# mLSTM and two expert layers on one Trainium2 core: the denominators' absolute values in PSUM, and other durations and ready times in the planner

## The chip, the cores and the metric

The kernel runs on one core of a Trainium2 chip. A core has a matrix engine (TensorE, PE in the rows; PEld is its weight load), three engines for elementwise work (VectorE, DVE; ScalarE, ACT; GpSimd, POOL) and a queue of DMA issues (SyncE, SP). The metric is the device time of one execution in microseconds (us); the time of a kernel is the median of several executions.

## The reference

An mLSTM over 4 batches and 8 heads, 768 steps, 40 columns a head; its output goes through two layers of the form `activation(x @ w_in) @ w_out`.

```python
for t in range(S):
    m_new = np.maximum(f_gate[:, :, t] + m, i_gate[:, :, t])
    f_stab = np.exp(f_gate[:, :, t] + m - m_new)
    i_stab = np.exp(i_gate[:, :, t] - m_new)
    C = f_stab * C + i_stab * np.einsum('bhd,bhe->bhde', vt, kt)
    n = f_stab * n + i_stab * kt
    h_tilde = np.einsum('bhde,bhe->bhd', C, qt)
    nq = np.einsum('bhd,bhd->bh', n, qt)
    denom = np.maximum(np.abs(nq), 1.0)
    y[:, :, t] = sigmoid(o_gate) * h_tilde / denom
...
h = x @ w_in;  x = (h - np.tanh(h)) @ w_out            # first layer, 320 -> 2048 -> 320
h = x @ w_in;  x = quadratic_relu(h) @ w_out           # second layer
```

## The kernel before

The 768 steps are cut into 6 chunks of 128. A *job* is one chunk of one batch, 24 in all, numbered chunk by chunk. A job loads q, k, v and o (`qkraw`, `nat`, `q3`) and its rows of the decay factors (`fb`, `gb`), and computes: decays by two scans on DVE (`d`, L456), scores on PE (`t_s`, L469, from job 12 on L485), scores times decays on DVE (L489), the matmul with the carried state (`t_n`, L521) and the matmul with the values (`t_n`, L530, the *value matmul* below). Then comes the chain that the change touches: the denominators of `t_n` through an absolute value on ACT (L537), a maximum with 1 on DVE (L538) and a reciprocal on DVE (L539), all 128x8; o times the reciprocal on POOL (L540); the product with `t_n` on DVE (`x`, L547); its transposes on PE (`t_x`, L552), and the splitting of `t_x` into high and low halves (L602 to L607). The state for the next chunk is built from `t_c` (L559) on ACT and DVE (L567 to L576).

From job 12 on q and k are split into halves before the scores (`xf`): ACT scales (L480), POOL subtracts for one half, DVE for the other (L482).

The layers run in 24 steps of 16 over blocks of 512 tokens (a *step* is one block with 128 columns of the hidden layer): 8 matmuls `h` (L630), an activation on ACT (L648) and DVE (L649), the high part on ACT (`gh`, L660) and the low part on DVE (`gl`, L661), and two steps later 12 matmuls `a` (L681) that read `gh` and `gl`. The first 8 steps of the first block (`wide`) have 3 `h` (L623) and 4 `a` in full precision; their weights `wf` are put together on ACT (`wf`, `cvb`, L316) and DVE (L318, L320), two instructions on each engine for a weight tile. The steps of the first layer run between the jobs of the next block; the second layer has no jobs beside it.

The order is made by a planner (`Plan`). Every operation has an engine, a duration in ns and a priority; `schedule` starts operations one after another on each engine by their ready time and priority, and the order of starts is the order in which they are issued. All engines then work off their instructions in that order, whatever the chip's real times are. An operation with `lock=True` takes its turn on one resource that DVE and POOL share in the plan. Idle time of PE before the first step is filled with dummy matmuls (`spare`, L769).

The decay factors of the later chunks go through DRAM: DVE ends them by a scan (`gr`, L381) and a memset (`fr`, L384), SP stores them (`gr_d`, `fr_d`), and SP loads them broadcast (`gb`, `fb`). On POOL, `gb` is copied in part to `gw` (L512, L513) and multiplied into `q3` (L506, L508), which L521 reads.

Of the kernel before, what the change touches and what calls it, by code (L numbers as in the profile page):

```python
# [69 lines left out]
class Op:  # L70
    __slots__ = ("eng", "ns", "prio", "fn", "allocs", "bufs", "preds", "succs", "left", "est", "start", "end", "seq", "out", "fill", "lock")


class Plan:
# [20 lines left out]
    def op(self, eng, ns, prio, fn, r=(), w=(), out=None, lock=False):  # L95
# [3 lines left out]
        o.bufs, o.fill, o.lock = [], 0, lock  # L99
# [114 lines left out]
def act(n, more=0):  # L214
    return 186 + n / 1.2 + 60 * more
# [12 lines left out]
def mlstm_moe_moe(ctx: ExitStack, tc: tile.TileContext, ig, fg, qk, qk3, q3, nat, w1, w2, cst, out):  # L228
# [107 lines left out]
    def gates(g, prio):  # L336
# [11 lines left out]
        op("DVE", 60, prio, lambda: nc.vector.tensor_copy(m_sb[:, 0:1], carry[:, g:g + 1]), [("carry", g)], [m_sb])  # L348
# [53 lines left out]
    def job(n, at, ld):  # L402
# [499 lines left out]
```

## Time and profile before

| | us |
|---|---|
| median of 3 executions | 820.48 (819.66 to 822.74) |
| the profiled execution | 822.96 |
| its span, first to last instruction | 821.2 |
| PE busy | 806.8 |
| DVE busy | 601.8 |
| ACT busy | 431.1 |
| POOL busy | 156.3 |

The span is the profiled execution less 1.8 us around it. Matmuls are pipelined, and a matmul that follows another closely is counted from its own start, so PE's busy time can hold short stalls; the waits of the rows below are times in which PE had nothing in flight.

### The profile page before, as it was taken

Reading aid. Unit: us, or ns where it says so; the run is one execution under the profiler, and the core shown is the slowest. Engines: PE = TensorE matmul, PEld = TensorE weight load, DVE = VectorE, ACT = ScalarE, POOL = GpSimd, SP = SyncE. Lnnn points to the kernel's source line nnn. Section 1 sums busy time; section 2 is a strip of 40 time slices with the busy share of each in tenths; the row PEclk is TensorE's granted clock in tenths of the full one; section 3 lists DMA queues with packets and bytes.
Section 4 is the critical chain, followed back from the end, with each engine's and each line's share of the span. In section 5 each row is a group of like instructions: output and inputs, shape, how many; then the busy total and the mean of one; then the engine's idle time right before and its main releaser. Section 6 shows DMA issues by size and latency. Waiting matters only on the chain.

```text
span 821.2 us, 15205 instructions
## 1 busy us (share of the span) xinstructions
PE 806.8 (98%) x6030; PEld 704.4 (86%) x6034; DVE 601.8 (73%) x922; ACT 431.1 (53%) x804; POOL 156.3 (19%) x179
## 2 busy tenths in 40 slices
PE   8999999999999999999999999999999999999998
PEld 6566887888988888888899989999999999999997
DVE  6999988879998898998666675565655655655654
ACT  4866764675676766654355543443433533433332
POOL 3253122315333332532020100100100100100000
PEclk9999999999999999999999999999999999999999
DMA  8889266576777767772263130100200000000000
GB/s 291 288 255 289 97 189 163 156 238 169 205 191 208 203 167 196 195 221 74 77 179 105 55 71 1 39 34 1 71 1 1 32 1 1 33 1 1 33 1 32
DMA packets 62978, 93.65 MB, mean 114 GB/s; under 512 B 4700, under 2 KB 45500, under 8 KB 62908
## 3 DMA queue, kind: packets, MB, share of 16 engines
q1 hardware_dynamic: 62860, 92.66, 38.7%
q8 instruction: 47, 0.77, 0.4%
q14 instruction: 23, 0.19, 0.1%
q10 hardware_dynamic: 48, 0.03, 0.0%
HBM read 78.88 MB, written 13.80 MB: 113 GB/s over the span
## 4 chain that ended last, share of the span: by engine, by line
PE 83%; DMA 7%; DVE 7%; issue 2%; ACT 1%; SPq 1%; POOL 0%; ACTq 0%; DVEq 0%; POOLq 0%
PE a L681 37%; PE h L630 36%; PE h L623 3%; DMA w_d<-w 3%; DMA w<-in_w_dram 2%; PE t_n L530 1%; PE t_n L521 1%; DVE d L456 1%; PE t_s L485 1%; DVE gl L661 1%; PE t_s L469 1%; DMA nat<-in_nat_dram 1%; PE t_x L552 1%; DMA gb<-gr_d 1%; PE t_c L559 1%
## 5 line engine op out<-in xcount | busy, mean ns | idle before, releaser
L630 PE MATMUL h<-x,w 128*128 128x512 f32 x1472 | 382.4, 396 | 0.0
L681 PE MATMUL a<-w,gh 128*128 128x320 f32 x1472 | 330.4, 310 | 0.2
L630 PEld LDWEIGHTS h<-x,w 128*128 128x128 f32 x1472 | 265.8, 188 | 44.9
L681 PEld LDWEIGHTS a<-w,gh 128*128 128x128 f32 x1472 | 253.7, 188 | 15.3 <-issue 0.6
L681 PE MATMUL a<-w,gl 128*128 128x320 f32 x736 | 227.9, 310 | 1.5 <-DVE gl L661 1.5
L661 DVE TENSOR_TENSOR gl<-g,gh 128x512 fp32r<-128x512 f32 x184 | 138.4, 753 | 82.1 <-ACT gh L660 80.9
L660 ACT CAST gh<-g 128x512 fp32r<-128x512 f32 x184 | 113.8, 619 | 114.6 <-DVE g L657 70.9
L681 PEld LDWEIGHTS a<-w,gl 128*128 128x128 f32 x736 | 138.5, 188 | 2.2 <-DVE gl L661 1.8
L655 ACT ACTIVATE g<-g,half 128x512 f32<-128x512 f32 x96 | 69.4, 723 | 127.7 <-DVE g L653 127.4
L657 DVE TENSOR_TENSOR g<-h,g 128x512 f32<-128x512 f32 x96 | 66.4, 692 | 73.5 <-ACT g L655 72.7
L649 DVE TENSOR_TENSOR g<-h,g 128x512 f32<-128x512 f32 x88 | 60.1, 682 | 31.8 <-ACT g L648 31.5
L648 ACT ACTIVATE g<-h 128x512 f32<-128x512 f32 x88 | 52.4, 596 | 57.2 <-PE h L630 56.9
L739 POOL TENSOR_TENSOR x<-xl,x 128x512 fp32r<-128x512 f32 x18 | 23.5, 1332 | 275.4 <-ACT x L734 275.0
L653 DVE TENSOR_SCALAR g<-h 128x512 f32<-128x512 f32 x96 | 66.2, 690 | 1.9 <-PE h L630 1.8
L456 DVE TENSOR_TENSOR_SCAN d<-fb,scan_id 128x512 f32<-128x512 f32 x40 | 56.9, 1432 | 0.0
L482 POOL TENSOR_TENSOR xf<-qkraw,xf 120x1024 fp32r<-120x1024 f32 x12 | 30.8, 2571 | 53.8 <-ACT xf L480 45.6
L480 ACT ACTIVATE xf<-qkraw,cs 120x512 fp32r<-120x512 f32 x48 | 32.4, 716 | 9.5 <-PE t_s L485 9.4
L489 DVE TENSOR_TENSOR d<-t_s,d 128x512 f32<-128x512 f32 x48 | 31.7, 679 | 4.6 <-PE t_s L485 3.4
L540 POOL TENSOR_TENSOR nat<-nat,dn 128x320 f32<-128x320 f32 x24 | 22.7, 947 | 58.3 <-DVE dn L539 58.3
L316 ACT ACTIVATE cvb<-w,half 128x704 bf16<-128x704 int8 x32 | 30.1, 941 | 4.7 <-DVE w L318 3.9
L496 POOL TENSOR_TENSOR nat<-nat,isT 128x328 f32<-128x328 f32 x24 | 20.3, 860 | 57.2 <-DMA nat<-in_nat_dram 27.4
L316 ACT ACTIVATE w<-w,half 128x704 f32<-128x704 int8 x24 | 22.6, 941 | 6.0 <-DMA w_d<-w 5.0
(98 smaller groups left out, 684.9 us busy)
## 6 DMA issues: line engine op xcount, KB each, us to landing
w<-in_w_dram SPq DMA_DIRECT2D x32, 703.6 KB
nat<-in_nat_dram SPq DMA_DIRECT2D x24, 484.0 KB
qkraw<-in_qk_dram SPq DMA_DIRECT2D x24, 480.0 KB
fb<-fr_d SPq DMA_DIRECT2D x40, 256.0 KB
w_d<-w SPq DMA_DIRECT2D x16, 352.0 KB
w<-w_d SPq DMA_DIRECT2D x16, 352.0 KB
qkraw<-in_qk_dram SPq DMA_DIRECT2D x24, 160.0 KB
xr_d<-xo SPq DMA_DIRECT2D x24, 160.0 KB
```

The source lines that it names most:

```text
L316: op("ACT", 935, prio, lambda o=o, y=y: nc.scalar.activation(o(), x(), AF.Relu, bias=rebase, scale=y * 2.0 ** 27), [t, "half"], [u if y > ...
L456: op("DVE", dve(1024), p, lambda o=dk[u][0], i=f[u][0]: nc.vector.tensor_tensor_scan(out=o(), data0=i(), data1=scan_id, initial=0.0, op0=A ...
L480: op("ACT", act(512, 1), at(u - 1), lambda raw=raw, t=t, z=z, cols=cols: nc.scalar.activation(t[:, cols], raw[:, cols], AF.Copy, scale=cs[ ...
L630: op("PE", pe(n), prio, lambda i=i, c=c, s=s: nc.tensor.matmul(p[:, :n], w[:, c:c + 128], x[:, s, :n], start=(i == 0), stop=(i == 7)), [(w ...
L648: op("ACT", act(n), prio + 0.5 - FFN, lambda: nc.scalar.activation(t[:, :n], p[:, :n], AF.Tanh), [p], [t])
L649: op("DVE", dve(n), prio + 0.5 - FFN, lambda: nc.vector.tensor_tensor(out=t[:, :n], in0=p[:, :n], in1=t[:, :n], op=ALU.subtract), [p, t], [t])
L653: op("DVE", dve(n), prio + 0.5 - FFN, lambda: nc.vector.tensor_scalar(t[:, :n], p[:, :n], -1.0, 1.0, op0=ALU.max, op1=ALU.min), [p], [t])
L655: op("ACT", act(n, 1), prio + 0.5 - FFN, lambda: nc.scalar.activation(t[:, :n], t[:, :n], AF.Square, bias=half[:, 0:1], scale=0.5), [t, "h ...
L657: op("DVE", dve(n), prio + 0.5 - FFN, lambda: nc.vector.tensor_tensor(out=t[:, :n], in0=p[:, :n], in1=t[:, :n], op=ALU.max), [p, t], [t])
L660: op("ACT", act(n), prio + 1 - FFN, lambda: nc.scalar.copy(gh[:, :n], t[:, :n]), [t], [gh])
L661: low = lambda e: e.tensor_tensor(out=gl[:, :n], in0=t[:, :n], in1=gh[:, :n].bitcast(F32), op=ALU.subtract)
L681: op("PE", pe(DM) if gl is not None else 2 * pe(DM, 128, 2), prio, lambda A=A, r=r, a=a, c=c, i=i, dt=dt: nc.tensor.matmul(A[:, 0:DM], a[: ...
```

## The change

There are three parts. The absolute value on ACT is written to columns 384 to 391 of the PSUM bank of `t_n` instead of to the SBUF tile `dn`, and the maximum on DVE reads it there and writes `dn`; the reciprocal stays in SBUF. The planner's durations are replaced for several operations (POOL's, three small DVE copies, ACT's operations with a scale, the value matmul). And `slack` is new: the ready time of a PE operation is put off by 600 ns after its last input for `t_x` and by 400 ns for the scores from job 12 on.

```diff
+SLACK = [600.0, 400.0, 0.0]
...
-                    s.est = max(s.est, o.end + (self.FAR if s.eng == "PE" else self.NEAR))
+                    s.est = max(s.est, o.end + (self.FAR + s.slack if s.eng == "PE" else self.NEAR))
...
-    return 186 + n / 1.2 + 60 * more
+    return 186 + n / 1.2 + 110 * more
...
-                        t[:, h * L:(h + 1) * L], start=True, stop=True), [t], [sp[u]])
+                        t[:, h * L:(h + 1) * L], start=True, stop=True), [t], [sp[u]], slack=SLACK[1])
...
-        op("POOL", pool(H * E1), at(1), lambda: nc.gpsimd.tensor_tensor(
+        op("POOL", 740, at(1), lambda: nc.gpsimd.tensor_tensor(
...
-                op("POOL", 530, at(1), lambda: nc.gpsimd.tensor_copy(gw[:, 0:2], g[:, 0:2, L - 1]), G, [gw])
+                op("POOL", 190, at(1), lambda: nc.gpsimd.tensor_copy(gw[:, 0:2], g[:, 0:2, L - 1]), G, [gw])
...
-        op("PE", 355 + 2 * H * 38, at(4), pv, [dk[0][1], dk[1][1], V], [p])
+        op("PE", 900, at(4), pv, [dk[0][1], dk[1][1], V], [p], slack=SLACK[2] if n >= FIRST else 0.0)
...
-        op("ACT", 180, at(5), lambda: nc.scalar.activation(dn.t, pn()[:, :, D], AF.Abs), [p], [dn])
-        op("DVE", 170, at(5), lambda: nc.vector.tensor_scalar_max(dn.t, dn.t, 1.0), [dn], [dn])
+        op("ACT", 180, at(5), lambda: nc.scalar.activation(p[:, 384:384 + H], pn()[:, :, D], AF.Abs), [p], [(p, "d")])
+        op("DVE", 175, at(5), lambda: nc.vector.tensor_scalar_max(dn.t, p[:, 384:384 + H], 1.0), [(p, "d")], [dn])
...
-                px[:, k * L:(k + 1) * L], x[:, k * 128:(k + 1) * 128], ident), [x, (x, "z"), "cs"], [px])
+                px[:, k * L:(k + 1) * L], x[:, k * 128:(k + 1) * 128], ident), [x, (x, "z"), "cs"], [px], slack=SLACK[0] if n >= FIRST else 0.0)
```

With one line more at the top, a line of the code after has a number one higher than the same line before (L538 is L539 after).

The order changes nearly everywhere in the first 420 us. Three places follow.

**The start, DVE, from the product x of job 2 to that of job 3.** `dn_528` before and `dn_520` after are job 3's denominators; L318 and L320 (L319 and L321 after) put weight tiles together. Before:

```order
L547 TENSOR_TENSOR x_108<-t_n_395,nat_156 128x320
L318 TENSOR_TENSOR wf_384<-wf_384,cvb_442 128x704
L320 SCALAR_TENSOR_TENSOR wf_384<-w64_256,wf_384 128x704
L538 TENSOR_SCALAR dn_528<-dn_528 128x8
L539 RECIPROCAL dn_528<-dn_528 128x8
L547 TENSOR_TENSOR x_108<-t_n_489,nat_209 128x320
```

After:

```order
L548 TENSOR_TENSOR x_108<-t_n_395,nat_154 128x320
L321 SCALAR_TENSOR_TENSOR wf_283<-w64_171,wf_283 128x704
L319 TENSOR_TENSOR wf_383<-wf_383,cvb_429 128x704
L539 TENSOR_SCALAR dn_520<-t_n_482 128x8
L540 RECIPROCAL dn_520<-dn_520 128x8
L321 SCALAR_TENSOR_TENSOR wf_383<-w64_256,wf_383 128x704
L319 TENSOR_TENSOR wf_447<-wf_447,cvb_522 128x704
L321 SCALAR_TENSOR_TENSOR wf_447<-w64_285,wf_447 128x704
L548 TENSOR_TENSOR x_108<-t_n_482,nat_209 128x320
```

Three weight instructions moved in between the reciprocal and the product of job 3; by that product DVE has done six of them where it had done four.

**Job 8, DVE, from its maximum to its product x, and SP's issues for jobs 8 and 9.** `g_1650` is the activation of the step then in work, `gl_1680` its low part, `fb_1565` the decays of job 9, `xo` the output of the first block. DVE before:

```order
L538 TENSOR_SCALAR dn_1634<-dn_1634 128x8
L649 TENSOR_TENSOR g_1650<-h_1567,g_1650 128x512
L539 RECIPROCAL dn_1634<-dn_1634 128x8
L456 SCALAR_TENSOR_TENSOR d_1671<-fb_1565,scan_id_73 128x512
L661 TENSOR_TENSOR gl_1680<-g_1650,gh_1669 128x512
L692 STREAM_TRANSPOSE xo_1624<-a_617 128x10x32
L692 STREAM_TRANSPOSE xo_1624<-a_624 128x10x32
L547 TENSOR_TENSOR x_108<-t_n_1577,nat_1025 128x320
```

DVE after:

```order
L539 TENSOR_SCALAR dn_1620<-t_n_1552 128x8
L662 TENSOR_TENSOR gl_1625<-g_1550,gh_1605 128x512
L540 RECIPROCAL dn_1620<-dn_1620 128x8
L693 STREAM_TRANSPOSE xo_1614<-a_651 128x10x32
L457 SCALAR_TENSOR_TENSOR d_1644<-fb_1526,scan_id_73 128x512
L457 SCALAR_TENSOR_TENSOR d_1656<-fb_1542,scan_id_73 128x512
L330 TENSOR_TENSOR w2_1496<-wf_447,w2_1496 128x704
L693 STREAM_TRANSPOSE xo_1614<-a_656 128x10x32
L693 STREAM_TRANSPOSE xo_1614<-a_661 128x10x32
L577 SCALAR_TENSOR_TENSOR C_1683<-C_797,gw_1522,t_c_1608 120x123 x2
L650 TENSOR_TENSOR g_1685<-h_1632,g_1685 128x512
L548 TENSOR_TENSOR x_108<-t_n_1552,nat_1015 128x320
```

The low part of the step that is in work stands ahead of both scans after, and behind a scan before. SP before (`w64` is a weight tile of 703.6 KB for the second layer; `gb_1435` and `gb_1480` belong to jobs 8 and 9):

```order
L282 DMA gr_d_79<-gr_1382 32x128
L282 DMA fr_d_78<-fr_1075 32x128
L282 DMA nat_1412<-in_nat_dram 128x968
L282 DMA w64_1421<-in_w2_dram 128x5629
L282 DMA gb_1435<-gr_d_79 40x3x128
L282 DMA fb_1444<-fr_d_78 128x4x128
L282 DMA fb_1457<-fr_d_78 128x4x128
L282 DMA gb_1435<-gr_d_79 40x3x128
L282 DMA gb_1435<-gr_d_79 40x2x128
L282 DMA gb_1480<-gr_d_79 40x3x128 x2
L282 DMA gb_1480<-gr_d_79 40x2x128
```

SP after:

```order
L283 DMA gr_d_79<-gr_1402 32x128
L283 DMA fr_d_78<-fr_1029 32x128
L283 DMA nat_1422<-in_nat_dram 128x968
L283 DMA gb_1441<-gr_d_79 40x3x128
L283 DMA fb_1451<-fr_d_78 128x4x128
L283 DMA fb_1456<-fr_d_78 128x4x128
L283 DMA gb_1441<-gr_d_79 40x3x128
L283 DMA gb_1441<-gr_d_79 40x2x128
L283 DMA gb_1475<-gr_d_79 40x3x128 x2
L283 DMA gb_1475<-gr_d_79 40x2x128
L283 DMA fr_1489<-in_fg_dram 32x128
L283 DMA ig_1493<-in_ig_dram 32x128
```

The weight load moved from ahead of the `gb` loads to behind them.

**Job 14, PE, from the step whose activation DVE works off last before the product x (`h_3058` before, `h_3116` after) to `t_x`.** Before:

```order
L630 MATMUL h_3058<-x1_1710,w9_931 128x512 x8
L681 MATMUL a_2647<-w7_1910,gh_2980 128x320 x2
L681 MATMUL a_2647<-w7_1910,gl_3017 128x320
L681 MATMUL a_2657<-w7_1910,gh_2980 128x320 x2
L681 MATMUL a_2657<-w7_1910,gl_3017 128x320
L681 MATMUL a_2661<-w7_1910,gh_2980 128x320 x2
L681 MATMUL a_2661<-w7_1910,gl_3017 128x320
L681 MATMUL a_2678<-w7_1910,gh_2980 128x320 x2
L681 MATMUL a_2678<-w7_1910,gl_3017 128x320
L630 MATMUL h_3111<-x1_1710,w10_966 128x512 x2
L552 MATMUL t_x_3119<-cs_72,x_108 128x128 x3
```

After:

```order
L631 MATMUL h_3116<-x1_1733,w10_985 128x512 x8
L682 MATMUL a_2634<-w8_840,gh_3074 128x320 x2
L682 MATMUL a_2634<-w8_840,gl_3129 128x320
L682 MATMUL a_2642<-w8_840,gh_3074 128x320 x2
L682 MATMUL a_2642<-w8_840,gl_3129 128x320
L682 MATMUL a_2657<-w8_840,gh_3074 128x320 x2
L682 MATMUL a_2657<-w8_840,gl_3129 128x320
L682 MATMUL a_2674<-w8_840,gh_3074 128x320 x2
L682 MATMUL a_2674<-w8_840,gl_3129 128x320
L631 MATMUL h_3163<-x1_1733,w11_1031 128x512 x8
L553 MATMUL t_x_3180<-cs_72,x_108 128x128 x3
```

Between the two stand 12 `a` and 2 `h` before, 12 `a` and 8 `h` after.

## Rows read from the trace of the kernel before

**Rows 1.** Busy time by stretch: us, PE, PEld, DVE, ACT, POOL, clock, DMA, GB/s.

```profile
32.90:120.00 87.10, 86.86 (x682) 63.66 (x682) 80.61 (x127) 64.25 (x122) 23.80 (x33) 1.00 0.69 212
200.00:420.00 220.00, 214.60 (x1914) 189.96 (x1913) 190.25 (x285) 130.05 (x262) 72.34 (x73) 1.00 0.62 172
```

**Rows 2.** What PE waited for, whole span: us in total, times, longest.

```profile
PE t_x L552 <- DVE x L547: 4.2, 4, 1.5
PE a L681 <- DVE gl L661: 1.5, 1, 1.5
...
PE t_s L485 <- DVE x L607: 1.1, 2, 0.9
...
PE t_n L521 <- POOL q L508: 0.2, 1, 0.2
```

**Rows 3.** The same columns as rows 1, around 130 us.

```profile
128.00:131.10 3.10, 1.46 (x8) 0.99 (x8) 3.10 (x6) 0.20 (x1) 1.02 (x2) 0.99 0.36 81
131.10:134.50 3.40, 3.40 (x14) 3.26 (x14) 2.54 (x7) 1.21 (x3) 0.31 (x2) 0.51 0.95 222
```

**Rows 4.** Timeline at job 8: start us, us, engine, instruction, idle before and releaser.

```profile
127.10 2.14 DVE L456 TENSOR_TENSOR_SCAN d<-fb,scan_id 128x512 f32<-128x512 f32 x1
...
127.43 0.72 POOL L540 TENSOR_TENSOR nat<-nat,dn 128x320 f32<-128x320 f32 x1
...
129.16 0.66 DVE L661 TENSOR_TENSOR gl<-g,gh 128x512 fp32r<-128x512 f32 x1
...
129.88 0.41 PE L681 MATMUL a<-w,gl 128*128 128x320 f32 x1 [1.54 <-DVE gl L661]
```

**Rows 5.** The maximum and the reciprocal: durations in ns, least/median/most; POOL's L482 beside them.

```profile
L538 DVE TENSOR_SCALAR dn<-dn x24: 140/172/2400, 14.8 to 401.5; 128x8 f32<-128x8 f32 x24
...
L539 DVE RECIPROCAL dn<-dn x24: 193/203/205, 15.0 to 401.7; 128x8 f32<-128x8 f32 x24
...
L482 POOL TENSOR_TENSOR xf<-qkraw,xf x12: 2387/2464/3107, 151.0 to 385.2; 120x1024 fp32r<-120x1024 f32 x12
```

**Rows 6.** Groups by line: busy us, mean ns of one.

```profile
L648 ACT ACTIVATE g<-h 128x512 f32<-128x512 f32 x88 | 52.4, 596 | 57.2 <-PE h L630 56.9
...
L538 DVE TENSOR_SCALAR dn<-dn 128x8 f32<-128x8 f32 x24 | 19.9, 829 | 4.9 <-ACT dn L537 4.7
```

**Rows 7.** Timeline at jobs 12, 14 and 17: POOL and DVE, and PE's wait.

```profile
198.56 3.01 DVE L661 TENSOR_TENSOR gl<-g,gh 128x512 fp32r<-128x512 f32 x1
...
238.79 0.67 DVE L649 TENSOR_TENSOR g<-h,g 128x512 f32<-128x512 f32 x1
...
240.01 0.52 PE L552 MATMUL t_x<-cs,x 128*128 128x128 f32 x3 [0.80 <-DVE x L547]
...
292.12 2.37 DVE L538 TENSOR_SCALAR dn<-dn 128x8 f32<-128x8 f32 x1
```

**Rows 8.** The chain that ended last, pieces: start us, us, what.

```profile
108.97 5.09 DMA w<-in_w_dram
114.07 6.60 DMA gb<-gr_d
...
146.41 1.84 PE h L630 x8
148.25 1.75 PE a L681 x12
```

**Rows 9.** Timeline of the start, ACT, DVE and PE.

```profile
29.84 0.93 ACT L316 ACTIVATE cvb<-w,half 128x704 bf16<-128x704 int8 x1
...
31.20 0.49 DVE L547 TENSOR_TENSOR x<-t_n,nat 128x320 f32<-128x320 f32 x1 [0.83 <-POOL nat L540]
31.61 0.88 DVE L318 TENSOR_TENSOR wf<-wf,cvb 128x704 int32<-128x704 f32 x1
...
32.87 7.99 PE L623 MATMUL h<-xf,wf 128*128 128x512 f32 x18
```

**Rows 10.** Timeline of PE at job 8's matmul with the carried state.

```profile
122.73 0.45 PE L521 MATMUL t_n<-C,q 80*128 80x82 f32 x2 [0.15 <-POOL q L508]
```

More of the change, by code (lines that the diff above doesn't have):

```diff
@@ L70 @@
 class Op:
-    __slots__ = ("eng", "ns", "prio", "fn", "allocs", "bufs", "preds", "succs", "left", "est", "start", "end", "seq", "out", "fill", "lock")
+    __slots__ = ("eng", "ns", "prio", "fn", "allocs", "bufs", "preds", "succs", "left", "est", "start", "end", "seq", "out", "fill", "lock", "slack")
 class Plan:
@@ L93, in buf, with op @@
         return b
-    def op(self, eng, ns, prio, fn, r=(), w=(), out=None, lock=False):
+    def op(self, eng, ns, prio, fn, r=(), w=(), out=None, lock=False, slack=0.0):
         o = Op()
@@ L98, in op @@
         o.allocs, o.preds, o.succs = [], set(), []
-        o.bufs, o.fill, o.lock = [], 0, lock
+        o.bufs, o.fill, o.lock, o.slack = [], 0, lock, slack
         key = lambda x: x if isinstance(x, tuple) else (x, None)
@@ L347, in gates @@
         load(ld, lambda: i_sb[0:32, 0:n], lambda: ig[:, cols], n / 8, w=[i_sb], rows=n * 4, eng="ACT" if g == 0 else "SP")
-        op("DVE", 60, prio, lambda: nc.vector.tensor_copy(m_sb[:, 0:1], carry[:, g:g + 1]), [("carry", g)], [m_sb])
+        op("DVE", 140, prio, lambda: nc.vector.tensor_copy(m_sb[:, 0:1], carry[:, g:g + 1]), [("carry", g)], [m_sb])
         op("DVE", dve(2 * n), prio, lambda: nc.vector.tensor_tensor_scan(
@@ L352, in gates @@
         if g + 1 < len(GROUPS):
-            op("DVE", 60, prio, lambda: nc.vector.tensor_copy(carry[:, g + 1:g + 2], m_sb[:, n:n + 1]), [m_sb], [("carry", g + 1)])
+            op("DVE", 140, prio, lambda: nc.vector.tensor_copy(carry[:, g + 1:g + 2], m_sb[:, n:n + 1]), [m_sb], [("carry", g + 1)])
         for o, d, f in ((fr, 0, ALU.add), (fr, 1, ALU.subtract), (i_sb, 1, ALU.subtract)):
@@ L501, in job @@
         if not last:
-            op("POOL", pool(DM), at(4), lambda: nc.gpsimd.tensor_tensor(
+            op("POOL", 725, at(4), lambda: nc.gpsimd.tensor_tensor(
                 out=nt[:, 0:DM].rearrange("p (h e) -> p h e", e=D), in0=nt[:, 0:DM].rearrange("p (h e) -> p h e", e=D),
@@ L505, in job @@
         if c > 0:
-            op("POOL", pool(256), at(0), lambda: nc.gpsimd.tensor_tensor(
+            op("POOL", 745, at(0), lambda: nc.gpsimd.tensor_tensor(
                 out=q[:, 0:2], in0=q[:, 0:2], in1=g[:, 0:2], op=ALU.mult), [(q, 0), *G], [(q, 0)], lock=True)
-            op("POOL", pool(128), at(0), lambda: nc.gpsimd.tensor_tensor(
+            op("POOL", 580, at(0), lambda: nc.gpsimd.tensor_tensor(
                 out=q[0:80, 2], in0=q[0:80, 2], in1=g[0:80, 2], op=ALU.mult), [(q, 1), *G], [(q, 1)], lock=True)
@@ L511, in job @@
                 gw = abuf("gw", [120, 3], F32, 2)
-                op("POOL", 530, at(1), lambda: nc.gpsimd.tensor_copy(gw[:, 0:2], g[:, 0:2, L - 1]), G, [gw])
-                op("POOL", 440, at(1), lambda: nc.gpsimd.tensor_copy(gw[0:80, 2:3], g[0:80, 2, L - 1:L]), G, [gw])
+                op("POOL", 190, at(1), lambda: nc.gpsimd.tensor_copy(gw[:, 0:2], g[:, 0:2, L - 1]), G, [gw])
+                op("POOL", 190, at(1), lambda: nc.gpsimd.tensor_copy(gw[0:80, 2:3], g[0:80, 2, L - 1:L]), G, [gw])
         p = jbank(n, "n", "t_n")
@@ L738, in layer2_x @@
             h = (y, "x", i // 2 * 2)
-            op("POOL", pool(n), prio + 4.5, lambda i=i: nc.gpsimd.tensor_tensor(
+            op("POOL", 1310, prio + 4.5, lambda i=i: nc.gpsimd.tensor_tensor(
                 out=plain(y[:, 4 if i == 2 else 2 + i, :n]), in0=order(t[:, i, :n]), in1=plain(y[:, 4 if i == 2 else i, :n]).bitcast(F32),
```

2 lines of the change are left out of this document (1 added, 1 removed).

## The prediction

> **What bounds the kernel now.** I read the busy times by stretch first, then the list of what PE waited for, then timelines at each wait. PE bounds the kernel: of the 87.1 us from 32.9 to 120 it is busy 86.86, of the 220 us from 200 to 420 it is busy 214.6 [rows 1], and nothing on the other engines costs time unless PE waits for it. So a change that adds no PE work and takes none away is worth what PE's waits are worth. They are few [rows 2]: 4.2 us at `t_x` for the product x on DVE, in four waits; 1.5 us at one `a` matmul for its low part `gl`; 1.1 us at the scores from job 12 on, the longest 0.9; 0.2 us at L521. [...] And PE cannot start the first step before 32.87 us [rows 9].
>
> Why the waits come is in the timelines. DVE waits inside its instructions while POOL works. The maximum over 8 columns takes 172 ns in the median, yet 2400 at most [rows 5], 2.37 at 292 us [rows 7], about as long as POOL's L482 at its median of 2464 ns [rows 5]; its 24 instances take 19.9 us where 24 x 0.172 is 4.1 [rows 6], so 15.8 us of DVE's time are such waiting. The low part at 198.56 takes 3.01 us [rows 7], the scan at 127.10 takes 2.14 with a POOL product beside it, and the low part behind that scan ends late enough to stop PE for 1.54 us [rows 4].
>
> **The change part by part.** All sums are in the profiled execution's time, 822.96 us (span 821.2 and 1.8 around it). It lies 2.5 us above the median of 820.48, and I carry that distance over as it is; were it due to the stretch at half clock, the median would gain that much less, which the range takes in.
>
> *Absolute value and maximum in PSUM.* No instruction is added. No row shows a maximum with a PSUM source: its price lies between the 140 ns of the quickest L538 and the 205 of the slowest reciprocal [rows 5]; I take 0.17, the median, and it is off PE's path except through x. What goes is the wait for POOL, up to 15.8 us of DVE's time, since the reciprocal right behind the maximum never takes longer than 205 ns. That is no gain of PE by itself; it counts through the waits below. [...]
>
> *Wait for the low part at 130 us.* After, the low part of the step in work stands ahead of the scans of job 8 on DVE. I worked out a margin for each low part: the PE work that stands between the end of its step's `h` and its first use, in pieces of 1.84 us for 8 `h` and 1.75 for 12 `a` [rows 8], less the chain over g (0.60, [rows 6]), L649 (0.67, [rows 7]), the high part (as g), `gl` (0.66, [rows 4]) and what stands between on DVE. It is -1.3 us for the one that waited before, and no other is negative; after, the smallest of the 88 is +0.7. So the 1.54 us go, and with them the stretch at half clock: 3.40 us at 0.51 hold 1.7 us of full speed work, so it cost 1.7. **Term A: -3.2** (bounds -3.2 and 0, if another low part waits instead).
>
> *Later `t_x`.* The same arithmetic for x: in job 14 PE has 12 `a` and 2 `h` between the `h` whose g1 DVE works off last and `t_x`, 1.75 + 0.46 = 2.2 us; the chain needs 0.60 + 0.67 + 0.49 for x [rows 6, 7, 9] and some 0.3 of hand-overs, 2.1. The margin of 0.15 was not enough: PE waited 0.80 [rows 7], so DVE was about 0.95 late. After it is 12 `a` and 8 `h`, 3.6 us, a margin of 1.5. The four jobs that waited are 12, 14, 15, 18, by 1.5, 0.8, 1.5 and 0.3 us at margins of 0.9, 0.15, 0.5, 0.85; their delays were thus 2.4, 0.95, 2.0 and 1.2. After their margins are 1.1, 1.5, 0.85 and 1.2, and over jobs 6 to 22 the smallest is 0.2 (job 6), where it was -1.7 before. With the same delays 1.3 and 1.15 us of waiting stay, 2.4 of 4.2; with DVE rid of the maximum's waits perhaps none. **Term B: -3.0**, between -1.8 and -4.2; 0 if delays grow by what the margins grew.
>
> *Later scores.* Two waits of 1.1 us in all, each put off by 0.4 us of other PE work: 0.9 becomes 0.5, the other goes. **Term C: -0.6** (0 to -1.1).
>
> *The start.* DVE has six weight instructions done by x of job 3, where it had four: 2 x 0.88 = 1.8 us more [rows 9]. Of that its idle 0.83 ahead of x covers a part, and the waits of the maxima that go (0.66 a piece on average, 829 less 172 ns [rows 6]) up to 1.0 more. ACT has two more of them (0.93 each [rows 9]) ahead of the last copy that the first step waits for. PE's part is dummy matmuls. So the first step starts between 0.1 earlier and 1.9 later; I take the middle. Nothing absorbs it, since from 32.9 to 120 PE waits for 0.24 us [rows 1]; the weights that are done earlier were not waited for. **Term D: +0.8.**
>
> *Job 8's q.* In the order DVE's memset of the first gates (L384) comes later: from it to job 8's L521 stand 13.2 us of PE work before, 9.7 after, 3.5 less for store, load and POOL's products. PE waited there already, 0.15 [rows 10]. In return the weight load moves from ahead of the `gb` loads to behind them; it took 5.09 us, and the last `gb` was issued when it had landed and took 6.60 [rows 8]. Credit between 0 and 5.1, taken as 2.5; the wait is then 0.2 + 3.5 - 2.5 = 1.2. **Term E: +1.0** (-0.2 to +3.5).
>
> *The other durations* (POOL's, small copies, the value matmul) act through the order alone, which the margins hold. Sum: -3.2 - 3.0 - 0.6 + 0.8 + 1.0 = **-5.0**, that is 817.96 for a profiled execution and 815.5 for the median.
>
> **The rivals.**
> *All waits go*: the maximum no longer holds DVE up and the credit of E is full: A -3.2, B -4.2, C -1.1, D 0, E -0.2, sum -8.7, 811.8. For it: 15.8 us of freed DVE time. Against: low parts and scans wait for POOL as before.
> *The waits change places*: the clock stays up, but another low part waits 1.5, and jobs 12 and 15 wait as now. A -1.7, B 0, C 0, D +0.8, E 0: -0.9, 819.6. For it: every order meets a different sequence on POOL, and job 12 waited at a margin of 0.9.
> *The maximum still waits with a PSUM source*: then B is -1.8, the sum -3.8, 816.7. Against: products with PSUM beside POOL, such as L649 at 0.67 [rows 7], show none of it.
> *Slower, the port's wait passes to the low part.* In jobs 12 to 20 POOL's L482 (2.46 us [rows 5]) runs as the value matmul ends. The maximum waited for it; now DVE goes on and comes to a low part or scan behind, and takes 3.01 instead of 0.66, 2.35 more [rows 7], ahead of x. At margins of about 1.15 that is a wait of 1.2 us in each of nine jobs, 10.8 where there were 4.2: +6.6; with A, D and E as above (C 0) +5.2, 825.7. It decides from five such jobs on: then 6.0 - 4.2 - 3.2 + 0.8 + 1.0 is about 0. Against: before, the maximum's 2.4 us were lost in the same place in five jobs, and none of those waited. [...]
>
> **How the numbers follow.** A measurement of this kernel tells 0.5% from no change, 4.1 us: faster is below 816.4, slower above 824.6. Forecast 0.43, with 813.5 to 817.5 of its own; all waits go 0.12; changed places 0.32 (817.5 to 822); maximum still waits 0.05; slower 0.08. Of the forecast seven tenths lie below 816.4, of the others 0.12 and some 0.05: faster 0.47. Slower 0.10, the rival and the end of the changed places. Within 0.5%: 0.43. The range from 811 to 822 leaves out the slower rival, a little of the changed places and the lower end of the best case, under 0.2.
>
> **What would show it.** Right: L538's most at about 0.2 us; no stretch of half clock near 130 us; waits at `t_x` of 0.5 to 2.5 us in all; the first `h` near 33.7 us; one wait of about 1.2 at job 8's L521. Wrong: low parts or scans of 2.5 us and more in the jobs from 12 on, and `t_x` behind them; a first step after 35 us; a wait of 3 us at job 8's q with the clock falling after it; or a `gl` at which PE waits again.

## The result and the profile after

The changed kernel is slower by 0.5%: median 824.43 us of 20 executions (819.97 to 831.74) against 820.65 before; ratio 1.0051, 95% interval 1.0033 to 1.0070. Forecast were 815.5 and a range of 811 to 822. The profiled execution took 827.70 (span 825.9). Times of the changed kernel scatter more than those of before (817.5 to 825.7), and the profiled execution is 3.3 us above the median.

What PE waited for after, to be held against [rows 2] (us in total, times, longest):

```profile
PE h L631 <- DVE w L330: 3.5, 1, 3.5
...
PE t_s L486 <- DVE x L608: 1.2, 1, 1.2
PE t_x L553 <- DVE x L548: 0.9, 2, 0.5
...
PE t_n L522 <- POOL q L507: 0.6, 1, 0.6
```

The wait for `gl` is gone and `t_x` fell from 4.2 to 0.9 us, as meant. A wait that was not there before is the longest: 3.5 us for `w` of L330. That instruction makes the low half of a weight tile for the next block, and the `h` of a step needs it for its last three matmuls.

By stretch, in the columns of [rows 1], the last two around that wait:

```profile
120.00:165.00 45.00, 40.47 (x415) 35.18 (x414) 38.66 (x61) 22.05 (x52) 18.59 (x25) 0.92 0.62 163
...
200.00:420.00 220.00, 217.30 (x1992) 192.55 (x1991) 178.59 (x286) 131.04 (x268) 72.42 (x73) 1.00 0.62 173
```

```profile
131.00:134.05 3.05, 0.00 (x0) 0.00 (x0) 3.05 (x3) 0.21 (x2) 2.25 (x3) 0.76 0.53 155
134.05:139.60 5.55, 5.55 (x16) 4.78 (x17) 4.49 (x10) 2.75 (x4) 0.48 (x1) 0.51 0.71 142
```

From 200 to 420 us PE is idle for 2.7 us where it was 5.4 [rows 1]. From 120 to 165 it is idle for 4.5, and 5.55 us pass at a granted clock of 0.51 of full speed (half clock), which cost another 2.7. The kernel before was idle for 2.0 us there and had 3.40 us at half clock [rows 3]; its row for the stretch is this:

```profile
120.00:165.00 45.00, 42.99 (x435) 37.24 (x433) 38.62 (x67) 24.75 (x57) 15.59 (x23) 0.96 0.62 163
```

The timeline at that place (DVE, POOL and PE, start us, us):

```profile
124.00 0.73 POOL L497 TENSOR_TENSOR nat<-nat,isT 128x328 f32<-128x328 f32 x1
...
124.15 3.20 DVE L662 TENSOR_TENSOR gl<-g,gh 128x512 fp32r<-128x512 f32 x1
...
124.70 0.72 POOL L503 TENSOR_TENSOR nat<-nat,wc 128x320 f32<-128x320 f32 x1
...
125.38 1.42 POOL L497 TENSOR_TENSOR nat<-nat,isT 128x328 f32<-128x328 f32 x2
...
128.85 2.80 DVE L457 TENSOR_TENSOR_SCAN d<-fb,scan_id 128x512 f32<-128x512 f32 x2
...
131.57 2.43 DVE L330 TENSOR_TENSOR w<-wf,w 128x704 fp32r<-128x704 f32 x1
...
131.85 0.72 POOL L541 TENSOR_TENSOR nat<-nat,dn 128x320 f32<-128x320 f32 x1
...
132.53 0.71 POOL L503 TENSOR_TENSOR nat<-nat,wc 128x320 f32<-128x320 f32 x1
...
134.05 1.65 PE L631 MATMUL h<-x,w 128*128 128x512 f32 x3 [3.49 <-DVE w L330]
```

The `gl` at 124.15 begins beside POOL's products and ends only 0.55 us after POOL pauses at 126.80: 3.20 us instead of 0.69. Behind it stand a few short instructions and two scans, then L330, which meets the next burst (a row of POOL products without a pause) and takes 2.43 instead of 0.88. PE waits for it.

The start, DVE and POOL, then ACT and PE, to be held against [rows 9]:

```profile
30.47 0.20 DVE L540 RECIPROCAL dn<-dn 128x8 f32<-128x8 f32 x1
30.59 0.84 DVE L321 SCALAR_TENSOR_TENSOR wf<-w,wf 128x704 int32<-128x704 int32 x1
30.76 1.26 POOL L541 TENSOR_TENSOR nat<-nat,dn 128x320 f32<-128x320 f32 x1 [3.02 <-DVE dn L540]
...
31.35 1.41 DVE L319 TENSOR_TENSOR wf<-wf,cvb 128x704 int32<-128x704 f32 x1
...
32.80 0.89 DVE L321 SCALAR_TENSOR_TENSOR wf<-w,wf 128x704 int32<-128x704 int32 x1
...
33.60 0.48 DVE L548 TENSOR_TENSOR x<-t_n,nat 128x320 f32<-128x320 f32 x1
33.64 1.78 ACT L317 ACTIVATE wf<-w,half 128x704 f32<-128x704 int8 x2
...
35.30 0.48 ACT L589 COPY xf<-t_x 128x384 f32<-128x384 f32 x1
...
35.84 0.70 PE L624 MATMUL h<-xf,wf 128*128 128x512 f32 x1 [0.44 <-ACT xf L589]
```

The first `h` starts at 35.84, 2.97 us later than before: x is 2.4 later, and the copy waits 0.55 more behind two weight instructions on ACT. This differs between executions: in the other profiles of orders that have this start it is at 34.53 to 36.47, in those of the order before at 32.35 to 33.02.

The maximum does what was said of it (least/median/most ns):

```profile
L539 DVE TENSOR_SCALAR dn<-t_n x24: 123/166/168, 15.4 to 408.8; 128x8 f32<-128x8 f32 x24
```

### The profile page after: what moved, and what is told of

Its sections match the earlier page's. It is cut to its first block, busy times and chain, and to the rows that moved or that the text cites. A ratio compares the mean times of both kernels' runs of the same rounds, so it can differ in the third digit from the quotient of the medians.

```text
span 825.9 us, 15221 instructions
## 1 busy us (share of the span) xinstructions
PE 809.4 (98%) x6035; PEld 705.8 (85%) x6038; DVE 586.7 (71%) x922; ACT 431.6 (52%) x804; POOL 160.9 (19%) x179
## 4 chain that ended last, share of the span: by engine, by line
PE 86%; DVE 6%; DMA 4%; issue 2%; ACT 1%; POOL 1%; SPq 0%; ACTq 0%; POOLq 0%
PE h L631 37%; PE a L682 37%; PE h L624 3%; DMA w_d<-w 2%; PE t_s L470 2%; PE t_n L531 2%; PE t_n L522 1%; DVE gl L662 1%; PE t_c L560 1%; PE t_s L486 1%; PE t_f L448 1%; PE spare L770 1%; DVE d L457 1%; PE t_x L553 1%; DVE w L321 1%
## 5 line engine op out<-in xcount | busy, mean ns | idle before, releaser
L649 ACT ACTIVATE g<-h 128x512 f32<-128x512 f32 x88 | 52.4, 596 | 61.5 <-PE h L631 61.3
L457 DVE TENSOR_TENSOR_SCAN d<-fb,scan_id 128x512 f32<-128x512 f32 x40 | 53.8, 1350 | 1.1 <-DMA fb<-fr_d 1.1
L507 POOL TENSOR_TENSOR q<-q,gb 120x256 f32<-120x256 f32 x20 | 19.6, 982 | 82.8 <-DMA q<-in_q_dram 70.1
L541 POOL TENSOR_TENSOR nat<-nat,dn 128x320 f32<-128x320 f32 x24 | 20.4, 850 | 67.4 <-DVE dn L540 57.1
## 6 DMA issues: line engine op xcount, KB each, us to landing
w<-in_w_dram SPq DMA_DIRECT2D x32, 703.6 KB
```

Source lines behind the costliest of these rows:

```text
L457: op("DVE", dve(1024), p, lambda o=dk[u][0], i=f[u][0]: nc.vector.tensor_tensor_scan(out=o(), data0=i(), data1=scan_id, initial=0.0, op0=A ...
L649: op("ACT", act(n), prio + 0.5 - FFN, lambda: nc.scalar.activation(t[:, :n], p[:, :n], AF.Tanh), [p], [t])
```

## Experiments

All times are medians, and ratios are to the kernel before with their 95% interval; before itself measured 820.2 to 820.9 beside them. The intervals reach 1.3 to 2.5 us to either side, so that two runs that differ by less than some 2 us are not told apart. Where instructions were moved, the order of all others is that of the kernel named. The kernels with moves (start, low weights) have line numbers six higher than after, those with the edit of `gl` one or two, those with both up to eight.

### The PSUM edit alone, and taken out

```diff
-        op("ACT", ... nc.scalar.activation(dn.t, pn()[:, :, D], AF.Abs), [p], [dn])
-        op("DVE", ... nc.vector.tensor_scalar_max(dn.t, dn.t, 1.0), [dn], [dn])
+        op("ACT", ... nc.scalar.activation(p[:, 384:384 + H], pn()[:, :, D], AF.Abs), [p], [(p, "d")])
+        op("DVE", ... nc.vector.tensor_scalar_max(dn.t, p[:, 384:384 + H], 1.0), [(p, "d")], [dn])
```

On the kernel before:

> The kernel before with one edit: the absolute value goes to PSUM and the maximum reads it there; planner and order of all instructions stay those of before. Theory A (the edit frees DVE and x comes earlier): the maximum takes 0.17 us in all 24 jobs, DVE's busy time falls by some 15 us, PE's waits at t_x fall from 4.2 to between 1 and 2.5 us, the wait for gl near 130 us and the half clock behind it stay; 1.7 to 3.2 us faster than before, 817.5 to 819 for a median of 820.65. Theory B (the waiting passes on to the next DVE instruction between two SBUF tiles): DVE's busy time falls by less than 6 us, t_x still waits about 4, time within 1 us of before. Theory C (the edit itself is what makes the changed kernel slower): 2 us or more slower than before.

Measured: 821.04, ratio 1.0015 (0.9992 to 1.0039): no difference that can be told. PE's waits, and one place in the timeline:

```profile
PE t_x L552 <- DVE x L547: 2.8, 5, 1.4
PE t_s L485 <- DVE x L607: 1.6, 2, 1.3
```

```profile
216.24 2.39 POOL L482 TENSOR_TENSOR xf<-qkraw,xf 120x1024 fp32r<-120x1024 f32 x1
216.25 0.17 DVE L538 TENSOR_SCALAR dn<-t_n 128x8 f32<-128x8 f32 x1
...
216.97 2.21 DVE L661 TENSOR_TENSOR gl<-g,gh 128x512 fp32r<-128x512 f32 x1 [0.32 <-ACT gh L660]
...
218.59 0.90 POOL L508 TENSOR_TENSOR q<-q,gb 80x128 f32<-80x128 f32 x1
```

DVE's busy time falls by 11.3 us (601.8 to 590.5), between theories A and B: 16 us go at the maximum, some 5 come back at others (2.4 at `gl`, 2.4 at the scans). The rows show how: the maximum passes beside L482 in 0.17 us, and the next `gl` is held instead.

Taken out of the changed kernel (the same two lines, the other way round):

> The changed kernel with the absolute value and the maximum back in the SBUF tile dn; all planner numbers and the order stay those of after. Theory A (the edit helps, the order is what costs): DVE's busy time rises by some 15 us to 600, single maxima take 2.4 us, t_x waits 1 to 3 us more, the time is 0 to 3 us above that of after, 824.4 to 827.5. Theory B (waiting only passes around): within 1 us of after, 824.4. Theory C (the edit is what makes after slower): back to 820 to 821.

Measured: 827.29, ratio 1.0082 (1.0052 to 1.0112). By the medians the edit was worth some 3 us in this order, but the intervals overlap; DVE's busy time rose by 9.2. Theory C is out: the edit does not make the kernel slower. The waits on weights and on x are there without it too:

```profile
PE t_x L553 <- DVE x L548: 3.8, 3, 2.9
PE h L631 <- DVE w L330: 2.0, 1, 2.0
```

### Moving the two places in the order

`x` of job 3 moved on DVE, and the copy behind it on ACT:

```diff
...
     P.schedule()
+    N = P.named
+    P.shift([("or", 0, 1), ("sub", 0, 2), ("or", 0, 2)], N["x", 3])
+    P.shift([("A", 0, 3, -1.0), ("sub", 0, 3), ("or", 0, 3), ("A", 0, 5, 1.0), ("A", 0, 6, 1.0)], N["xf", 3])
+    N["t", 3, 0].fill = 5
```

(`shift` puts the named operations behind another one in the order of issue.)

> The changed kernel with one move in the order at the start: the product x of job 3 stands ahead of the three weight instructions that came between (DVE), and the copy of its transposes ahead of the three weight instructions of ACT behind which it stood; ten of the dummy matmuls ahead of the transposes are left out. Theory S (the start costs what x of job 3 is held up): x of job 3 starts near 31.4 us where it was 33.6, the first wide h starts near 33.1 where it was 35.84, and the whole is 2.5 us faster than after, 821.9. Rival (weights that come later are then waited for in the next steps, or the time is lost again at job 8): under 1 us faster, 823.5 or more.

Measured: 824.16, ratio 1.0038 (1.0015 to 1.0061). The first `h` started at 32.44, 3.4 us earlier, and the whole gained under 1 us: theory S is right on the place and wrong on what it is worth in this order. Its profile shows where the lead went: the third line below is a wait at 39.62 that no profile without this move has, the second is L330 again (its old number plus six) with half clock behind it (0.66 from 130 to 135 us), the first is mainly x of job 9.

```profile
PE t_x L559 <- DVE x L554: 3.6, 2, 3.0
PE h L637 <- DVE w L336: 2.5, 1, 2.5
PE h L630 <- DVE gh L651: 1.8, 1, 1.8
```

Now the low half of the weight tile that PE had waited for, moved ahead of the scans:

```diff
...
     P.schedule()
+    P.shift([("lo", 0, 2)], P.named["gl", 16])
```

> The changed kernel with one move in the order near 130 us: the low half of one weight tile (L330, the instruction for which PE waited 3.49 us at 134.05) stands right behind the low part gl at 124.15, ahead of both scans of job 9. Theory L (that place in DVE's order is the cause): this wait goes, with it the half clock from 132 to 139.5 (2.8 us) or most of it; PE next waits some 1.5 us for x of job 8; 3 to 5 us faster than after, 819.4 to 821.4. Rival (DVE is late there by the contention with POOL, whatever stands first): another wait of 2 to 3.5 us takes its place, the clock falls again, under 1.5 us faster than after.

Measured: 824.34, ratio 1.0043 (1.0025 to 1.0061). The wait for L330 is gone, and another of 3 us stands some 17 us further on, at job 9:

```profile
146.37 4.62 DVE L668 TENSOR_TENSOR gl<-g,gh 128x512 fp32r<-128x512 f32 x1
146.73 0.72 POOL L547 TENSOR_TENSOR nat<-nat,dn 128x320 f32<-128x320 f32 x1
147.41 0.72 POOL L509 TENSOR_TENSOR nat<-nat,wc 128x320 f32<-128x320 f32 x1
148.09 2.35 POOL L489 TENSOR_TENSOR xf<-qkraw,xf 120x1024 fp32r<-120x1024 f32 x1
150.91 0.48 DVE L554 TENSOR_TENSOR x<-t_n,nat 128x320 f32<-128x320 f32 x1
...
151.54 0.71 PE L559 MATMUL t_x<-cs,x 128*128 128x128 f32 x3 [3.03 <-DVE x L554]
```

```profile
152.00:155.20 3.20, 3.20 (x11) 2.77 (x10) 2.66 (x5) 1.15 (x4) 0.22 (x2) 0.51 0.87 268
```

One `gl` is held through three POOL instructions and ends 0.55 us behind the last. The product x stands behind it, and half clock follows here too. The run with the start moved shows the same 4.62 (at 148.05) and a `t_x` wait of 3.0; in the profile of after that place cost 0.5. So in these two runs a gain ahead of job 9 is lost at job 9. It need not be: in the second profile of after (below) PE is as early at 130 us and waits 0.46 for that x. The rival, contention whatever stands first, fits: another wait took the place, the clock fell again, and nothing was won that can be told.

### The low part read from PSUM

```diff
-                out=t[:, :n], in0=p[:, :n], in1=t[:, :n], op=ALU.subtract), [p, t], [t])
+                out=p[:, :n], in0=p[:, :n], in1=t[:, :n], op=ALU.subtract), [p, t], [t])
+            src = p
...
-        op("ACT", act(n), prio + 1 - FFN, lambda: nc.scalar.copy(gh[:, :n], t[:, :n]), [t], [gh])
-        low = lambda e: e.tensor_tensor(out=gl[:, :n], in0=t[:, :n], in1=gh[:, :n].bitcast(F32), op=ALU.subtract)
+        op("ACT", act(n), prio + 1 - FFN, lambda: nc.scalar.copy(gh[:, :n], src[:, :n]), [t], [gh])
+        low = lambda e: e.tensor_tensor(out=gl[:, :n], in0=src[:, :n], in1=gh[:, :n].bitcast(F32), op=ALU.subtract)
```

> The changed kernel, the same order of all instructions, with one edit in the first layer: the activated tile is written back into the PSUM bank of h, from which gh and gl then read, so that gl has one PSUM and one SBUF source where it had two SBUF sources. Theory P (what costs PE its time from 120 to 160 us is gl held up for as long as POOL works without a break, 3.20 us in the profile of after at 124.15 and 4.62 at 146.4 where the low weights were moved): all 88 gl of the first layer take 0.64 to 0.75 us, DVE's busy time falls by 8 to 11 us, the wait for the low weights near 134 us goes or falls below 1 us, and with it the half clock; 3 to 6 us faster than after, 818.5 to 821.5. Rival (the waiting passes on to the next instruction between SBUF tiles, the scan or the weights' low half): DVE's busy time falls by less than 4 us, a wait of 2 us or more stays near 134 or 155 us, within 1.5 us of after.

Measured: 822.64, ratio 1.0012 (0.9991 to 1.0033). No `gl` of the first layer is held, there is no half clock (1.00 in every stretch up to 200 us), and DVE is busy for 569.5 us where it was 586.7: theory P's mechanism holds, and its size does not. The gain is 1.8 us of median where 3 to 6 were expected. One price I had not counted: the bank of `h` is free only after `gl`, and the next `h` waits for it. Job 8's q also cost 1.7 in this profile, where it was 0.6.

```profile
L664 DVE TENSOR_TENSOR gl<-h,gh x88: 637/684/693, 81.7 to 472.7; 128x512 fp32r<-128x512 f32 x88
```

```profile
PE h L631 <- DVE gl L664: 2.3, 2, 1.3
```

> The kernel before, the same order of all instructions, with the same one edit (the activated tile of the first layer in the PSUM bank of h, gh and gl read it there); the maximum stays in SBUF. Theory P: no gl over 0.8 us in the first layer; the wait for gl near 130 us stays in part, since the scan of 2.14 us ahead of it still waits; t_x waits fall by what the 3.01 us of the gl at 198.6 cost; 1 to 3 us faster than before, 817 to 819. Rival (as above): within 1 us of before, 819.5 to 821.

Measured: 819.16, ratio 0.9979 (0.9963 to 0.9996), within theory P's 1 to 3 us, with 2.0 us of waits for the bank.

> The kernel before in its own order with both edits: the maximum reads PSUM, and gl of the first layer too. Theory P (what the maximum no longer waits for is then waited for by the next gl or scan, so the one edit is worth something only with the other): t_x waits under 1 us in all, DVE's busy time 18 to 25 us below that of before; 1 us or more faster than with gl's edit alone (819.2), that is 816.5 to 818.2. Rival (the scans and weight tiles take the waiting over): 818.7 to 820.

Measured: 817.23, ratio 0.9960 (0.9943 to 0.9978). Alone the maximum's edit brought nothing that can be told; beside `gl`'s the median is 1.9 us lower, which fits theory P, but the intervals overlap and so it is not shown.

> The changed kernel with gl's edit and with x of job 3 moved ahead of the three weight instructions at the start. Theory S with P (the 2.4 us gained at the start were lost again in the earlier run because a gl met a burst of POOL at 148 us; with gl off the shared port they stay): no wait over 2 us near 150 us, 2 to 3 us faster than the changed kernel with gl's edit alone (822.6), 819.6 to 820.6. Rival (the end of the first layer's early jobs is set by loads, so that an earlier start is waited out in any case): within 1 us of 822.6, with a wait for q, a weight tile or x of 2 us or more between 40 and 160 us.

Measured: 818.97, ratio 0.9985 (0.9963 to 1.0007), 3.7 us under the changed kernel with `gl`'s edit alone by the medians, 0.27% by the ratios; the two intervals overlap. The first `h` starts at 31.88 and no wait over 1.0 us follows between 40 and 420 us, as theory S with P said; that the start's gain stays in the time is likely and not shown. The shared port is the planner's name for the one resource that DVE and POOL share in the plan; what it is on the chip no run shows, only that `gl` took 0.69 us at most with one source in PSUM and up to 4.62 with both in SBUF.

### Which of the planner's numbers

Slack alone, on the kernel before (the slack lines of the change, nothing else):

> The kernel before with the slack alone (600 ns for t_x, 400 ns for the scores from job 12 on); durations as before, denominators in SBUF. The order changes from the last jobs of the first block on. Theory D (the new durations are what makes the changed kernel slower): the slack does what it was forecast to do, t_x waits 1 to 2.5 us in place of 4.2, the start is that of before, 817 to 820. Rival (any new order meets POOL's bursts at other places and loses there about what it gains): 820 to 825, with a wait of over 1.5 us at another line or a half clock of more than 3.4 us.

Measured: 827.86, ratio 1.0082 (1.0054 to 1.0110): the rival, and worse than it. L330 took 2.96 us at 150.08 and PE waited 2.1 for it, with half clock behind (0.83 from 150 to 160 us). Another 2.0 us of waiting, at the scores at 64.30 (the clock averages 0.99 from 0 to 120 us), has no releaser in the profile; what it comes from stays open.

The next three runs set the slack of the changed kernel (`FIRST` is job 4, `STACK` job 12).

```diff
-SLACK = [600.0, 400.0, 0.0]
+SLACK = [0.0, 0.0, 0.0]
```

> The changed kernel without the slack (all three values zero): new durations, denominators in PSUM. Theory D: the start is that of after (first wide h near 35.5 us), and so 823 to 826, t_x waits 1 to 3 us more than in after. Rival (the slack moved job 8 into its bad place): the wait for the low weights is gone and the time is 820 to 822 in spite of the late start.

Measured: 821.99, ratio 1.0016 (1.0000 to 1.0032): the rival again. The start is late (35.01), yet between 120 and 160 us PE waits for nothing over 0.3 us. DVE's order has the same low half ahead of the scans there:

```profile
118.65 1.36 DVE L330 TENSOR_TENSOR w<-wf,w 128x704 fp32r<-128x704 f32 x1
```

It is the same tile's as the one at 131.57 after. `t_x` waits 4.1 us without slack, the other numbers being those of after.

```diff
-... [px], slack=SLACK[0] if n >= FIRST else 0.0)
+... [px], slack=SLACK[0] if n >= STACK else 0.0)
```

> The changed kernel with the 600 ns for t_x only from job 12 on (both slacks then begin where PE had waited in the kernel before); the order up to job 12 is that of the run without slack. Theory K (the slack is right for jobs 12 to 22 and does its damage in jobs 4 to 11, where no t_x had waited): first h at 35.0 us, no wait over 1 us and no half clock between 100 and 180 us, t_x waits after 180 us 1 to 2 us in place of the 4.1 of the run without slack; 818 to 821, below the 822.0 of the run without slack and the 824.4 of after. Rival (any new order costs about this much): 822 to 826, with a new wait of over 1.5 us or a half clock after 180 us.

Measured: 818.50, ratio 0.9967 (0.9947 to 0.9986). `t_x` waits 1.2 us in all, and once the steps run PE waits for no other engine longer than 0.5 us at a time.

The reverse (`FIRST <= n < STACK`, and zero for the scores):

> The reverse of the late slack: 600 ns for t_x in jobs 4 to 11 only, none after and none for the scores; the order up to job 12 is that of after. Theory K (the damage is done there): as late as after up to 200 us, with the wait for the low weights near 131 us or the t_x wait of job 9 near 151 and a half clock behind it, and from there the t_x waits of the run without slack (about 4 us): 824.5 to 828. Rival (the slack costs nothing by itself, the late jobs decide): 820 to 823.

Measured: 828.68, ratio 1.0107 (1.0081 to 1.0134).

```profile
PE t_x L553 <- DVE x L548: 6.8, 3, 3.3
PE h L631 <- DVE w L330: 1.5, 1, 1.5
```

The 6.8 us at `t_x` are 0.5 at the start, 3.0 at job 9 and 3.3 at 338.98, in a job that has no slack in this run; half clock follows the last two (0.56 from 152.7 to 156.0 us, then 0.62 over 4.0 us). In the profile without slack the late jobs' `t_x` waits are smaller and come to 3.6 us, so the one at 338.98 adds only its half clock, some 1.5 us (the 4.0 us at 0.62).

The four settings make a table that adds up: no slack 821.99; late (with the 400 ns at the scores) 3.5 less; early 6.7 more; both should then be 825.2, and after measured 824.43 and 823.83. Seen from the late slack's 818.50, the early slack costs 5.9. On the kernel before, with its old durations, both together cost some 7 us (827.86), so the sizes hold for this plan only. The late slack was not run with the old durations.

The profiles show where the early slack costs. Six have it, with these durations and `gl` in SBUF (the two of after, and the runs with the maximum in SBUF, the start moved, the low half moved and the early slack alone): each waits 1.5 to 3.5 us for L330 near 131 us, or 2.9 to 3.0 for x of job 9 near 152, or for both. The three without it (no slack, late slack, late slack with the start moved) wait for neither, and no `gl` of theirs takes over 1.23 us between 120 and 160 us.

### After once more, and what beats both

> The changed kernel once more, unchanged, for a second profile. Theory K and L: between 120 and 165 us PE loses 5 to 9 us again, to the low weights near 131 us or to x of job 9 near 151, each with a stretch of half clock behind it; the first wide h starts at 35.0 to 36.0 us; the median is 823 to 826. Rival (the 3.49 us of the profile were one bad execution): the second profile shows under 2 us of waits there and no half clock.

Measured: 823.83, ratio 1.0056 (1.0027 to 1.0085). The median is where theories K and L put it; the second profile is what the rival said, 1.9 us of waits between 120 and 165 us and no half clock there:

```profile
PE h L631 <- DVE w L330: 1.5, 1, 1.5
```

```profile
123.10 1.92 DVE L662 TENSOR_TENSOR gl<-g,gh 128x512 fp32r<-128x512 f32 x1
...
128.73 1.35 DVE L330 TENSOR_TENSOR w<-wf,w 128x704 fp32r<-128x704 f32 x1
```

The same wait at the same place, 1.5 us of it, and the clock kept at 1.00 there: with the same instructions in the same order POOL's burst had 1.38 us left when `gl` began, and 2.65 in the first profile; `gl` was held for 1.2 and 2.5 us. That execution took 822.8 us, 4.9 less than the first and as much as the profiled execution of before. It has half clock elsewhere, behind a wait of 1.8 us at the scores at 321.20 (0.66 over the next 4.8 us):

```profile
PE t_s L486 <- DVE x L608: 2.1, 2, 1.8
```

> The changed kernel with three edits together: the t_x slack only from job 12 on, x of job 3 ahead of the three weight instructions at the start, and the low parts of the first layer read from PSUM. If the places are independent (theory K for the slack, S for the start, P for the low parts): from the 818.5 of the late slack alone the start takes 2.0 to 2.5 us and the low parts 1 to 2, so 814 to 815.5, faster than all runs so far. Rival (the h bank that gl now holds longer, 2 us of PE's waits in the runs with gl's edit, and later x of job 4 onward eat it): 816.5 to 818.5.

Measured: 823.88, ratio 1.0038 (1.0023 to 1.0054): the places are not independent, and the time lies above even the rival's.

```profile
PE h L637 <- DVE gl L670: 6.5, 5, 3.0
```

In the order of the late slack `gl` stands further behind the `h` whose bank it holds: in its profile 5.45 us lie between the activation's product at 121.41 and its `gl` at 126.86, with two scans, two products of the scores and two transposes between them. Half clock is back behind one of the longest waits (0.59 from 126 to 130 us). Without `gl`'s edit:

> The changed kernel with the t_x slack only from job 12 on and x of job 3 ahead of the three weight instructions at the start; low parts as in after. Theory S (the start's 2.4 us are kept where no gl meets a burst of POOL between 100 and 160 us): 815.5 to 817 where the late slack alone measured 818.5. Rival (in this order too, an earlier PE brings a gl or a weight tile into a burst): 818 to 821, with a wait of over 1.5 us and a half clock between 100 and 180 us.

Measured: 816.84, ratio 0.9958 (0.9939 to 0.9977), no half clock (1.00 from 100 to 170 us), and by the medians 1.7 us under the late slack alone, though the intervals overlap. At 40.90 an `h` waits 1.8 us for `gh` (L651), as in every run with the moved start. This and the kernel before with both PSUM edits (817.23) are the fastest of the study; their intervals overlap.

## Why the prediction was wrong

**Term A, the low part at 130 us (-3.2): failed.** The margins for the 88 low parts held, PE waited for none of them. But the sentence "the 1.54 us go, and with them the stretch at half clock" took `gl` for the only product of DVE that could be late there. The low halves of the weights (L330) had no margin worked out, though my own fence of the order after shows one behind both scans. PE waited 3.49 and 1.47 us for it in two profiles, and in the first one half clock followed again: 6.2 us lost there where 3.2 had been. The margins also took every instruction at its undisturbed length (0.66 for `gl`), while my own rows had one of 3.01; here a `gl` of 3.20 made L330 late. They were a weak guide before already: for x the smallest was -1.7, at a job that did not wait, and the four that waited had 0.15 to 0.9. Nor does the half clock hang on the wait alone: with `gl`'s edit on the kernel before, PE waited 1.5 us at the same `a` and the clock stayed at 1.00 from 120 to 140 us.

**What moved it there: shown.** The slack of jobs 4 to 11, where PE had not waited at `t_x`. I had costed the slack only at the jobs that waited, and put everything else to "the order alone, which the margins hold". The runs put the price of the early slack at 6.7 us without the late one and 5.9 with it; that is most of the 8.9 between the forecast 815.5 and the 824.43. In the order that it makes, `gl` meets long rows of POOL products ahead of L330 and of x of job 9; moving L330 alone won nothing that can be told (824.34), and reading `gl` from PSUM won 1.8 of it (822.64), so the hold-up of `gl` beside POOL is a likely part of the price and the rest is open.

**Term B, later `t_x` (-3.0): right.** 4.2 became 0.9 us, forecast 1.2, and without slack it is 4.1; the late slack with the one at the scores is worth 3.5 us of time with nothing else changed.

**Term C (-0.6): wrong.** The wait at the scores is 1.2 us where it was 1.1, and 2.1 in the second profile, with half clock behind it.

**Term D, the start (+0.8): mis-sized, 2.97** (1.66 in the second profile). From the reciprocal to x passed 0.84 us before and 2.93 after, before with this reciprocal ahead of the x of [rows 9]:

```profile
30.16 0.20 DVE L539 RECIPROCAL dn<-dn 128x8 f32<-128x8 f32 x1
```

I had counted two weight instructions more by that x; what counts is that three stand between, and none before. I had credited waits of the maxima that go, up to 1.0 us; they came back at a weight instruction (1.41 beside POOL's product instead of 0.88). And the copy on ACT waited 0.55, which I had named and not added.

**Term E, job 8's q (+1.0):** the wait was 0.6 where 0.15 had been, so +0.4, within the bounds.

In the first profile the terms come to +3.0 - 3.3 + 0.1 + 3.0 + 0.4 = +3.2 of the 4.7 us by which it is longer; three smaller new waits (0.6 at `t_i`, 0.5 and 0.4 at `t_n`) make up the rest. The second profile is no longer than that of before, so one pair of profiles does not stand for the medians.

**The maximum in PSUM.** That it no longer waits was right; no row of before showed it, and the runs do: 168 ns at most after and 167 with the edit alone, where 2400 had been [rows 5]. That DVE is rid of the wait was not: of 16 us some 5 pass on to the next instructions between SBUF tiles. This was the slower rival's mechanism, given 0.08, in jobs 12 to 20; the port in its name is the planner's. The measured time is near its 825.7 by luck: low parts held by POOL do stand ahead of the long waits, but at jobs 8 and 9, and with the maximum back in SBUF these waits are there too (2.0 and 2.9 us, 827.29). A source in PSUM made neither instruction longer: the maximum's median is 166 ns against 172, that of `gl` 684 against 692. The 88 `gl` with one SBUF source took 0.69 us at most, those with two up to 4.62. The L649 of [rows 7] had no POOL product beside it (the last one ended at 238.22), but all 88 of that line, which read PSUM, took 0.69 us at most in the kernel before.

**The scatter.** Two profiles of the changed kernel wait 3.5 and 1.5 us in one place. Part of the spread of its 20 executions, 12 us, goes with the clock: of the 32 executions of both runs, 11 with a mean granted clock of 0.997 or less have a median of 828.4 us, 13 with 0.999 or more one of 822.5. These 13 still spread from 819.7 to 827.5. Which waits do this is not shown, since one execution of a run is profiled.

## What to carry to other kernels

Work out a margin for every product that the bounding engine waits for, weights included, with the lengths that instructions have beside the other engine, and put slack only where a wait was seen: here the same 600 ns were worth 3.5 us in the late jobs (with the 400 ns at the scores) and cost 6.7 in the early ones. The wait beside POOL that was taken from the maxima was met in part by the next instructions between SBUF tiles: of 16 us 11.3 stayed off DVE, and no time was won that can be told. That it is a gain once `gl` reads PSUM too is what the runs suggest (817.23 against 819.16), and their intervals overlap. A place that costs 3 us in a profile is not worth 3 us until the next place downstream has been seen without it.

## What the runs showed of the hardware

In the profiles of before and after, 26 of the `gl` of the first layer that the timelines list singly, each with two SBUF sources, took over 0.72 us. All 26 began beside a POOL product, and 22 ended 0.54 to 0.56 us after the end of one, often the last of a row; the other four stand beside products that the timelines list together. The one of 4.62 us lasted through three whole POOL instructions that end at 150.44 (low half moved). Elsewhere `gl` is let in between two, and then the second is longer: with the maximum alone in PSUM a `gl` ends at 219.18, 0.55 us after L482, and POOL's next product (L508) takes 0.90 us, where the 20 of before have a least of 0.45 and a median of 0.52. At 90.00 in the profile of after a `gl` takes 0.65 us, and the POOL product beside it 3.11. What decides between these is not shown. With one source in PSUM 88 of them took 0.64 to 0.69 us.

PE's granted clock after a wait: 3.49 us of waiting were followed by 5.55 us at 0.51 of full speed, 3.03 us by 3.20 us or more at 0.51, while 1.47 us in the second profile left it at 1.00 (131 to 135 us). The length of the wait alone does not decide: 1.54 us were followed by 3.40 us at 0.51 in the kernel before [rows 3], 1.5 us were not in that kernel with `gl`'s edit, where the clock was 1.00 from 120 to 140 us.
